# Loads behind a gate per tile, and another order in the second group, in a pooled-attention and expert-mixture kernel

## The chip, the core and the metric

The kernel runs on one core of a Trainium2 chip. The core has a matrix engine (TensorE, PE in the profile; its weight loads are shown as PEld), a vector engine (VectorE, DVE), a scalar engine (ScalarE, ACT), GpSimd (POOL) and SyncE (SP). Each works through its own list of instructions in order. Transfers between the chip's memory (DRAM) and the on-chip memory are made by 16 DMA engines, for which SP and POOL each issue work on a queue of their own. The metric is the device time of one execution in microseconds (us); lower is better.

## The reference

Eight batches of eight heads; 576 tokens of 64 numbers for each head. Keys and values are averaged over groups of 8 neighbouring tokens (72 pooled rows for a head), and every query attends to the 72 pooled rows of its head. The result, 4608 tokens of 512 numbers, goes through four small networks (512 to 1024 to 512), whose outputs are added with a token's own weights.

```python
k_p = k.reshape(B, H, Sp, pool, D).mean(axis=3)          # B 8, H 8, Sp 72, pool 8, D 64
v_p = v.reshape(B, H, Sp, pool, D).mean(axis=3)
scores = scale * np.matmul(q, k_p.transpose(0, 1, 3, 2))
scores = scores - np.max(scores, axis=-1, keepdims=True)
attn = np.exp(scores)
attn = attn / (np.sum(attn, axis=-1, keepdims=True) + 1e-09)
x = np.matmul(attn, v_p)                                 # then (4608, 512)
p = domain_probs / (domain_probs.sum(-1, keepdims=True) + 1e-09)
for e in range(4):
    h = np.maximum(x @ w1[e], 0.0)
    out += p[:, e:e + 1] * (h @ w2[e])
```

## The kernel before

**Tiles and steps.** The tokens are cut into 36 tiles of 128 (`t`), four tiles make a group (`g`, 512 tokens, nine groups). The networks run group by group and expert by expert: 36 steps `s = 4 g + e`. A step has 12 slots. In a slot TensorE does either two of the eight column blocks of the first matrix product of the *next* step (`up`, line 422; slots 0 and 1 of each three do one block each) or the second product of one tile of *this* step (`down`, line 454; the third slot), whose result VectorE weights and adds up (`collect`, line 466). After four experts the tile's sum is written out by SP (line 484).

**Attention beside it.** What a tile needs before its group's first step is hung into the slots by a hand-written plan: `at(slot, function, ...)` (line 490) puts a call behind the slot's products, and the final loop (line 588) calls what a slot has, in the order in which it was put there. There is no scheduler: each engine gets its instructions in exactly this order. `plan_tile` (line 501) hangs up the stages of one tile, and `plan_batch` (line 493) those of a batch's keys and values, with the batch's own loads `load_k` and `load_v` for the batch two later. From tile 8 on (group 2, called the body here) a tile's base slot is `(4 g - 5 + i) * 12`, so tiles follow each other 12 slots apart.

**Stages of a tile** in the body, with the slot counted from its base: `turn_q` (-6) turns the queries (`qT`) by a DMA transpose on SP; `scores` (0) is the product with the pooled keys on TensorE (line 306); `less_max` (0) on VectorE (lines 317 and 319); `expo` (+1) on ScalarE (line 329) writes `attn`; `attn_T` (+1) turns it (`attnT`) by a DMA transpose on SP (line 367); `sums` (+2) on VectorE (line 349 on); `context` (+6) is the product with the pooled values on TensorE (line 385), which VectorE scales into `x_sb` (line 391), and which SP turns into `xT` by a DMA transpose (line 405). `by_dma(t)` (line 284) tells body tiles, which turn by DMA, from tiles 0 to 7, which turn on TensorE with copies out of PSUM by ScalarE or VectorE (lines 296, 300, 371, 372).

**Stages of a batch**: `prep_k` folds the keys and pads them on VectorE (lines 225, 232, 240), `prep_kT` turns them four slots later, `prep_v` folds the values (lines 225, 232, 270) eight slots later. Two buffers each hold the raw keys and values.

**Loads.** All loads of queries, keys, values and weights are issued by POOL (lines 79, 83, 107, 115, 121), in the order of the calls. Loads convert from 32 to 16 bits on the way. A load waits only until its buffer is free: a key buffer until VectorE has folded the old keys, a query buffer (there are eight) until the old queries have been turned. POOL therefore runs ahead of the plan, and loads of the body start whenever the last one's buffer comes free. A load of keys or of values is two DMA issues, one of 512 rows and one of 64; a load of queries is one, or two where the tile lies over the border of two batches.

**Group 1** (tiles 4 to 7) is planned by itself, while the weights of the experts are still coming in: batch 1 from slot 10 on, tiles at slots 13, 17, 21 and 25.

Of the kernel before, what the change touches and what calls it, by code (L numbers as in the profile page):

```python
# [12 lines left out]
BF16 = mybir.dt.bfloat16  # L13
# [4 lines left out]
def kernel(  # L18
# [10 lines left out]
    nc = tc.nc  # L29

    B, H, S, D = q.shape
# [10 lines left out]
    TPG = G // P  # L42
    NT = NTOK // P
# [9 lines left out]
    const = ctx.enter_context(tc.tile_pool(name="const", bufs=1))  # L53
# [38 lines left out]
    def segments(t0, n):  # L92
        segs = []
        t = t0
        while t < t0 + n:
            b = t // S
            end = min(t0 + n, (b + 1) * S)
            segs.append((b, t - b * S, end - t, t - t0))
            t = end
        return segs  # L100
# [19 lines left out]
    def load_w2(e):  # L120
# [8 lines left out]
        out=dp0[:], in_=moe_domain_probs[0:G].rearrange("(p c) e -> p c e", c=TPG)  # L129
# [4 lines left out]
        out=dpr[:], in_=moe_domain_probs[G:NTOK].rearrange("(t p) e -> t p e", p=P)  # L134
# [7 lines left out]
        out=qg[:], in_=q[0][:, 0:G, :].rearrange("h (p c) d -> p h c d", c=TPG)  # L142
# [4 lines left out]
    for sign, base in ((1, 0), (-1, SP - 1)):  # L147
        nc.gpsimd.affine_select(
            out=own[:], in_=own[:], compare_op=ALU.is_ge, fill=0.0,
            base=base, channel_multiplier=sign,  # L150
# [8 lines left out]
    for c in range(TPG):  # L159
# [21 lines left out]
        out=p_sb[:, :, 0:TPG].rearrange("p e c -> p c e"), in0=dp0[:],  # L181
# [5 lines left out]
    for t in attn:  # L187
# [5 lines left out]
        out=mask_v[:].rearrange("p a z y d -> p (a z y) d"),  # L193
        in_=own[:].rearrange("p a z y -> p (a z y)").unsqueeze(2).to_broadcast(
            [P, NPAIR * 4, D]
        ),
# [3 lines left out]
        out=mask_k[:, 1:NPAIR], in0=mask_v[:, 1:NPAIR, 0], in1=mask_v[:, 0:NPAIR - 1, 1]  # L200
# [64 lines left out]
    def prep_v2(b):  # L265
        fold(vraw[b % 2], 0, NB, 2)
        s = last_fold(vraw[b % 2], "v")
        vbd[b] = prep.tile([P, NPAIR, 2, 2, D], BF16, name="vbd")
        for z in range(2):
            nc.vector.tensor_tensor(  # L270
                out=vbd[b][:, :, z],
                in0=s[:, z:z + NPAIR].unsqueeze(2).to_broadcast([P, NPAIR, 2, D]),
                in1=mask_v[:, :, z], op=ALU.mult,
            )
# [9 lines left out]
    def by_dma(t):  # L284
        return t >= 2 * TPG

    def turn_q(t):
        qT[t] = soft.tile([P, NPAIR, P], BF16, name="qT")
        if by_dma(t):
            nc.sync.dma_start_transpose(  # L290
                out=qT[t][:], in_=qrow[t][:].rearrange("p h d -> p (h d)")
            )
            return
        ps = ps_t.tile([P, NPAIR, P], BF16, tag="t", name="qT_ps")
        for pair in range(NPAIR):
            nc.tensor.transpose(
                ps[:, pair, :],
                qrow[t][:, 2 * pair:2 * pair + 2].rearrange("p h d -> p (h d)"), ident[:],
            )
        nc.scalar.copy(out=qT[t][:], in_=ps[:])  # L300
# [26 lines left out]
    def expo(t):  # L327
        if by_dma(t):
            nc.scalar.activation(  # L329
                out=attn[t % 2][:, 0:ROWS].rearrange("p (h j) -> p h j", j=SP),  # L330
                in_=st[t][:].rearrange("p g h j -> p (g h) j"),
                func=ACT.Exp, scale=EXP_SCALE,
            )
            return
        e_sb = soft.tile([P, H, SP], F32, name="e_sb")
        nc.scalar.activation(
            out=e_sb[:], in_=st[t][:].rearrange("p g h j -> p (g h) j"),
            func=ACT.Exp, scale=EXP_SCALE,
        )
        st[t] = e_sb  # L340

    rss = {}

    def sums(t):
        e = st[t][:]
# [15 lines left out]
            op0=ALU.mult, op1=ALU.mult,  # L361
        )

    def attn_T(t, copy=nc.vector.tensor_copy):
        attnT[t] = soft.tile([P, NB, P], BF16, name="attnT")
        if by_dma(t):
            nc.sync.dma_start_transpose(out=attnT[t][:], in_=attn[t % 2][:])
            return
        ps = ps_t.tile([P, NB, P], BF16, tag="t", name="at_ps")
        for i in range(NB):  # L370
            nc.tensor.transpose(ps[:, i, :], attn[t % 2][:, i * P:(i + 1) * P], ident[:])
        copy(out=attnT[t][:], in_=ps[:])
# [5 lines left out]
    def context_rows(t):  # L378
        ps = ps_t.tile([P, DM], F32, tag="t", name="x_ps")
        for b, _, n, at in segments(t * P, P):  # L380
            flat = vbd[b][:].rearrange("p a z y d -> p (a z y d)")
            for i in range(NB):
                c0, c1 = max(0, 4 * i - 1), min(4 * NPAIR, 4 * i + 2)
                h0 = max(0, 2 * i - 1)
                nc.tensor.matmul(  # L385
                    ps[at:at + n, h0 * D:(h0 + c1 - c0) * D],
                    lhsT=attnT[t][:, i, at:at + n], rhs=flat[:, c0 * D:c1 * D],
                    start=(i == 0), stop=(i == NB - 1), skip_group_check=True,
                )
        x_sb = soft.tile([P, DM], BF16, name="x_sb")  # L390
        nc.vector.scalar_tensor_tensor(  # L391
            out=x_sb[:].rearrange("p (h d) -> p h d", d=D),
            in0=ps[:].rearrange("p (h d) -> p h d", d=D), scalar=V_MEAN,
            in1=rss[t][:].unsqueeze(2).to_broadcast([P, H, D]),
            op0=ALU.mult, op1=ALU.mult,
        )
        return x_sb

    def context(t):
        g, col = t // TPG, (t % TPG) * P  # L400
        if t % TPG == 0:
            xT[g] = grp.tile([P, KC, G], BF16, name="xT")
        if by_dma(t):
            x_sb = context_rows(t)
            nc.sync.dma_start_transpose(out=xT[g][:, :, col:col + P], in_=x_sb[:])
            return
        ps = ps_t.tile([P, KC, P], F32, tag="t", name="x_ps")
        for pair in range(NPAIR):
            for b, _, n, at in segments(t * P, P):
                for z in range(2):  # L410
                    nc.tensor.matmul(  # L411
                        ps[:, pair, at:at + n],
                        lhsT=vbd[b][:, pair, z].rearrange("p y d -> p (y d)"),
                        rhs=attnT[t][:, pair + z, at:at + n],
                        start=(z == 0), stop=(z == 1),
                    )
        nc.scalar.copy(out=xT[g][:, :, col:col + P], in_=ps[:])
# [69 lines left out]
    SLOTS = 12  # L487
    plan = {}

    def at(slot, fn, *args):  # L490
        plan.setdefault(slot, []).append((fn, args))

    def plan_batch(b, slot):
        at(slot, prep_k, b)
        at(slot + 4, prep_kT, b)
        at(slot + 8, prep_v, b)
        if b + 2 < B:
            at(slot + 8, load_k, b + 2)
            at(slot + 8, load_v, b + 2)

    def plan_tile(t, slot, turn=0):
        exp, norm, move, sum_v = (3, 4, 3, 8) if by_dma(t) else (4, 5, 7, 9)
        if t + TPG < NT:
            at(slot, load_q, t + TPG)
        at(slot + turn, turn_q, t)
        at(slot + 2, scores, t)
        at(slot + 2, less_max, t)
        at(slot + exp, expo, t)
        at(slot + move, attn_T, t)
        at(slot + norm, sums if by_dma(t) else normalise, t)  # L510
        at(slot + sum_v, context, t)

    at(SLOTS - 4, domain_probs)
    plan_batch(1, SLOTS - 2)
    for i, slot in enumerate((1, 5, 9, 13)):
        plan_tile(TPG + i, SLOTS + slot)
    done_batches = 2
    for g in range(2, NG):
        for i in range(TPG):
            t = g * TPG + i  # L520
            base = (E * g - 5 + i) * SLOTS
            last_b = ((t + 1) * P - 1) // S
            if last_b >= done_batches:
                plan_batch(last_b, base - 13)
                done_batches += 1
            plan_tile(t, base - 2, -4)


    def split_q(c):
# [3 lines left out]
    def idle_products(n):  # L533
        ps = ps_o.tile([P, DM], F32, name="o_ps")
        for _ in range(n):
            nc.tensor.matmul(ps[:], lhsT=still[:, 0:P], rhs=still[:], start=True, stop=True)
# [17 lines left out]
    idle_products(5)  # L554
    normalise(0)
    prep_v2(0)
    attn_T(0, nc.scalar.copy)
    idle_products(2)
    context(0)
    less_max(1)  # L560
    expo(1)
# [5 lines left out]
    for t in range(1, TPG):  # L567
        if t == 1:
            turn_q(3)
        attn_T(t, nc.scalar.copy)  # L570
        if t + 1 < TPG:
            expo(t + 1)
        down(0, t - 1, 0, FB // 2)
        context(t)
        if t == 1:
            scores(3)
        down(0, t - 1, FB // 2, FB)
        up_tile(0, t)
        if t + 1 < TPG:
            normalise(t + 1)  # L580
        if t == 1:
            less_max(3)
        collect(0, t - 1)
# [4 lines left out]
    for s in range(NSTEP):  # L588
        for slot in range(SLOTS):
            part, i = slot % 3, slot // 3  # L590
# [39 lines left out]
```

## Time and profile before

| what | value |
|---|---|
| median of 3 runs | 569.9 us (569.69 to 571.6) |
| profiled execution | 573.24 us |
| its span, first to last instruction | 571.5 us |
| mean granted TensorE clock | 0.994 |
| busy share of PE, DVE, ACT, POOL | 95%, 47%, 36%, 11% |
| TensorE waits for attnT by DMA | 11.9 us, 6 times |
| TensorE waits for qT by DMA | 1.3 us, once |
| query loads in the span | 36 issues of 864 ns on POOL |
| DMA to landing, qT (min, median, max) | 2.4, 2.4, 7.7 us |
| DMA to landing, attnT (min, median, max) | 2.6, 2.6, 7.2 us |

A line of a timeline gives the start, the duration, the engine, the source line, the operation, what it writes and reads, and in brackets how long the engine had been idle and what it then waited for. SPq and POOLq are the queues on which DMA work is issued; the duration of a DMA issue is not that of the transfer, whose landing is given apart. A line of waits gives the total, the number and the longest. The granted clock is the share of TensorE's full clock that the chip let through.

### The profile page before, as it was taken

How to read it: one execution, taken by the hardware profiler on the slowest of the kernel's cores; microseconds unless marked ns; L12 is line 12 of the kernel's file. 1: busy time of each engine (PE TensorE's matmuls, PEld its weight loads, DVE VectorE, ACT ScalarE, POOL GpSimd, SP SyncE). 2: the span in 40 equal slices, each digit the busy share in tenths (PEclk: the TensorE clock that was granted, in tenths of full speed). 3: DMA queues.
4: the chain of work that ended last, by engine and by line, in shares of the span. 5: the costliest groups of instructions: out<-in, count | busy, mean ns of one | idle time of the engine just before them, and what ended most of it. 6: DMA issues, size and time to landing. Idle time of an engine off the chain costs nothing.

```text
span 571.5 us, 7185 instructions
## 1 busy us (share of the span) xinstructions
PE 540.4 (95%) x2888; PEld 259.2 (45%) x2888; DVE 269.2 (47%) x462; ACT 208.0 (36%) x347; POOL 64.2 (11%) x93
## 2 busy tenths in 40 slices
PE   3899898899898999899989999999999999999997
PEld 1564444344443444344444444444444444444443
DVE  4855865344552444544473444654465444422223
ACT  1564442233332333233333333333333333333330
POOL 7225303100040000300022000000000000000000
PEclk9999999899998999999999999999999999999999
DMA  9999998911592123781359243322221221111001
GB/s 140 207 203 200 197 110 135 121 22 30 98 160 37 30 31 104 106 86 31 86 102 108 36 75 74 50 38 68 68 42 31 59 76 30 31 34 50 1 0 73
DMA packets 111232, 45.43 MB, mean 79 GB/s; under 512 B 88128, under 2 KB 106560, under 8 KB 111200
## 3 DMA queue, kind: packets, MB, share of 16 engines
q0 software_dynamic: 52512, 22.55, 32.9%
q1 hardware_dynamic: 58688, 22.44, 17.2%
q8 instruction: 22, 0.36, 0.3%
q14 instruction: 10, 0.08, 0.0%
HBM read 45.16 MB, written 9.44 MB: 96 GB/s over the span
## 4 chain that ended last, share of the span: by engine, by line
PE 82%; DMA 8%; DVE 6%; issue 1%; ACT 1%; POOL 0%; POOLq 0%
PE o_ps L461 39%; PE h_ps L428 37%; DMA attnT<-attn 6%; PE x_ps L385 2%; PE sc L306 1%; DMA qg<-in_q_dram 1%; DMA qT<-qrow 1%; DVE mx L317 1%; DVE d_sb L319 1%; PE h_ps L444 1%; DVE kraw L225 1%; ACT attn L329 1%; PE x_ps L411 1%; DVE attn L357 1%; DVE es L349 0%
## 5 line engine op out<-in xcount | busy, mean ns | idle before, releaser
L432 ACT ACTIVATE h_sb<-h_ps 128x512 bf16<-128x512 f32 x280 | 166.4, 596 | 313.1 <-PE h_ps L428 313.1
L428 PE MATMUL h_ps<-xT,w 128*128 128x512 bf16 x1120 | 275.6, 380 | 0.0
L461 PE MATMUL o_ps<-w,h_sb 128*128 128x512 bf16 x1152 | 273.9, 381 | 0.0
L461 PEld LDWEIGHTS <-h_sb 128*128 128x128 bf16 x1152 | 112.8, 98 | 135.1 <-issue 3.6
L476 DVE SCALAR_TENSOR_TENSOR acc<-o_ps,p_sb,acc 128x512 f32<-128x512 f32 x108 | 81.0, 750 | 183.1 <-PE o_ps L461 183.1
L428 PEld LDWEIGHTS <-w 128*128 128x128 bf16 x1120 | 106.1, 98 | 116.9 <-issue 0.6
L472 DVE TENSOR_SCALAR acc<-o_ps,p_sb 128x512 f32<-128x512 f32 x36 | 27.0, 750 | 61.4 <-PE o_ps L461 61.4
L107 POOL DMA_DIRECT2D qrow<-in_q_dram x36 | 30.4, 864 | 83.2 <-DMA qT<-qrow 53.0
L317 DVE TENSOR_REDUCE mx<-sc 128x8 f32<-128x576 f32 x36 | 27.2, 755 | 12.1 <-PE sc L306 12.1
L391 DVE SCALAR_TENSOR_TENSOR x_sb<-x_ps,rs 128x512 bf16<-128x512 f32 x28 | 19.4, 691 | 26.2 <-PE x_ps L385 26.2
L319 DVE TENSOR_TENSOR d_sb<-sc,mx 128x576 f32<-128x576 f32 x36 | 27.3, 758 | 1.2
L79 POOL DMA_DIRECT2D kraw<-in_k_dram x9 | 6.8, 759 | 170.7 <-DVE k_sum L232 168.3
L385 PE MATMUL x_ps<-vbd,attnT 128*128 128x192 bf16 (+5 forms) x155 | 14.6, 234 | 11.9 <-DMA attnT<-attn 11.9
L329 ACT ACTIVATE attn<-d_sb 128x576 bf16<-128x576 f32 x28 | 19.1, 682 | 13.4 <-DVE d_sb L319 10.9
L349 DVE TENSOR_REDUCE es<-attn 128x8 f32<-128x576 bf16 x28 | 20.9, 746 | 0.5
L385 PEld LDWEIGHTS <-attnT 128*128 128x128 bf16 (+1 forms) x155 | 11.5, 101 | 20.5 <-DMA attnT<-attn 15.3
L306 PE MATMUL sc<-kT,qT 128*128 128x144 bf16 (+1 forms) x160 | 15.6, 232 | 1.6 <-DMA qT<-qrow 1.3
L306 PEld LDWEIGHTS <-qT 128*128 128x128 bf16 (+1 forms) x160 | 11.5, 102 | 11.4 <-DMA qT<-qrow 1.8
L225 DVE TENSOR_TENSOR kraw<-kraw 128x1280 bf16<-128x1280 bf16 (+5 forms) x18 | 10.8, 599 | 3.5 <-DMA kraw<-in_k_dram 3.2
L79 POOL DMA_DIRECT2D vraw<-in_v_dram x8 | 6.2, 773 | 39.0 <-DVE v_sum L232 35.5
L225 DVE TENSOR_TENSOR vraw<-vraw 128x1280 bf16<-128x1280 bf16 (+1 forms) x16 | 10.4, 653 | 0.2
L255 PE MATMUL kT_ps<-ident,kpad 128*128 128x128 bf16 x10 | 1.2, 264 | 9.2 <-DVE kpad L240 9.2
(61 smaller groups left out, 145.9 us busy)
## 6 DMA issues: line engine op xcount, KB each, us to landing
out_dram<-acc SPq DMA_DIRECT2D x36, 256.0 KB, 2.1
vraw<-in_v_dram POOLq DMA_DIRECT2D x8, 512.0 KB, 7.6
w<-in_moe_w_dram POOLq DMA_DIRECT2D x8, 512.0 KB, 16.0
w<-in_moe_w_dram POOLq DMA_DIRECT2D x4, 1024.0 KB, 16.8
kraw<-in_k_dram POOLq DMA_DIRECT2D x7, 512.0 KB, 6.0
qrow<-in_q_dram POOLq DMA_DIRECT2D x28, 128.0 KB, 8.0
kraw<-in_k_dram POOLq DMA_DIRECT2D x2, 256.0 KB, 4.4
kraw<-in_k_dram POOLq DMA_DIRECT2D x8, 64.0 KB, 5.6
```

The lines of the kernel that those rows point to most:

```text
L107: nc.gpsimd.dma_start(out=qrow[t][at:at + n], in_=q[b][:, tok:tok + n, :].rearrange("h p d -> p h d"),)
L225: nc.vector.tensor_add(out=rows[:, i0:i1, 0:w], in0=rows[:, i0:i1, 0:w], in1=rows[:, i0:i1, w:2 * w],)
L306: nc.tensor.matmul(sc[at:at + n, pair // 2, (pair % 2) * PW:(pair % 2 + 1) * PW], lhsT=qT[t][:, pair, at:at + n], rhs=kT[b][:].rearrange(" ...
L317: nc.vector.reduce_max(out=mx[:], in_=view, axis=AX.X)
L319: nc.vector.tensor_tensor(out=d_sb[:], in0=view, in1=mx[:].unsqueeze(3).to_broadcast([P, 2, 4, SP]), op=ALU.subtract,)
L329: nc.scalar.activation(out=attn[t % 2][:, 0:ROWS].rearrange("p (h j) -> p h j", j=SP), in_=st[t][:].rearrange("p g h j -> p (g h) j"), fun ...
L385: nc.tensor.matmul(ps[at:at + n, h0 * D:(h0 + c1 - c0) * D], lhsT=attnT[t][:, i, at:at + n], rhs=flat[:, c0 * D:c1 * D], start=(i == 0), s ...
L428: nc.tensor.matmul(ps[:], lhsT=w1_sb[e][:, kc, fb * P:(fb + 1) * P], rhs=xT[g][:, kc, :], start=(kc == 0), stop=(kc == KC - 1),)
L432: nc.scalar.activation(out=hs[s][:, fb, :], in_=ps[:], func=ACT.Relu)
L461: nc.tensor.matmul(ps[:], lhsT=hs[s][:, fb, i * P:(i + 1) * P], rhs=w2_sb[e][:, fb, :], start=(fb == 0), stop=(fb == FB - 1),)
L472: nc.vector.tensor_scalar_mul(out=accs[t][:], in0=ps[:], scalar1=p_sb[:, e, t:t + 1])
L476: nc.vector.scalar_tensor_tensor(out=accs[t][:], in0=ps[:], scalar=p_sb[:, e, t:t + 1], in1=accs[t][:], op0=ALU.mult, op1=ALU.add,)
```

## The change

- **A gate for each body tile.** After `context(t)`, POOL copies one element of that tile's `x_sb` into a scrap tile (`gate`). Since POOL works in order, loads called after it are issued only when `x_sb` is there.
- **Loads behind it.** In the body `load_q(t + 4)` is called behind the gate of tile `t` (slot +6) and not at the tile's slot -2. `load_k` and `load_v` of batches 4 to 7 are taken out of `plan_batch`; they go to a list, and each tile's gate lets one of them follow its query load.
- **Group 1.** Tiles are planned at slots 12, 16, 20 and 24 (one earlier) with `attn_T` and `context` one slot later within the tile, so that these two stay in the same slots; queries of tiles 5 to 7 are turned one slot ahead; batch 1's keys are turned at slot 12 and its values folded at slot 12 (14 and 18 before). The loads of batch 3's keys and values are called at slot 12, ahead of the queries of tiles 8 and 9. `attnT` of these tiles is copied by ScalarE and not by VectorE.
- **Tile 8** has its queries turned on TensorE instead of by DMA, two slots before its scores.

```diff
     def turn_q(t):
-        if by_dma(t):
+        if by_dma(t - 1):
...
+    gated = const.tile([1, 1], BF16, name="gated")
...
-    def attn_T(t, copy=nc.vector.tensor_copy):
+    def attn_T(t, copy=nc.scalar.copy):
...
-            x_sb = context_rows(t)
+            x_sb = x_sbs[t] = context_rows(t)
...
         at(slot + 8, prep_v, b)
-        if b + 2 < B:
-            at(slot + 8, load_k, b + 2)
-            at(slot + 8, load_v, b + 2)
+
+    def gate(t):
+        nc.gpsimd.tensor_copy(out=gated[:], in_=x_sbs.pop(t)[0:1, 0:1])
 
     def plan_tile(t, slot, turn=0):
-        exp, norm, move, sum_v = (3, 4, 3, 8) if by_dma(t) else (4, 5, 7, 9)
-        if t + TPG < NT:
+        exp, norm, move, sum_v = (3, 4, 3, 8) if by_dma(t) else (4, 5, 8, 10)
+        if t + TPG < NT and not by_dma(t):
             at(slot, load_q, t + TPG)
...
         at(slot + sum_v, context, t)
+        if by_dma(t):
+            at(slot + sum_v, gate, t)
+            if t + TPG < NT:
+                at(slot + sum_v, load_q, t + TPG)
 
-    plan_batch(1, SLOTS - 2)
-    for i, slot in enumerate((1, 5, 9, 13)):
-        plan_tile(TPG + i, SLOTS + slot)
-    done_batches = 2
+    at(SLOTS - 2, prep_k, 1)
+    at(SLOTS, prep_kT, 1)
+    at(SLOTS, prep_v, 1)
+    at(SLOTS, load_k, 3)
+    at(SLOTS, load_v, 3)
+    for i, slot in enumerate((0, 4, 8, 12)):
+        plan_tile(TPG + i, SLOTS + slot, -1 if i else 0)
+    done_batches, waiting = 2, []
...
                 plan_batch(last_b, base - 13)
                 done_batches += 1
-            plan_tile(t, base - 2, -4)
+                if last_b + 2 < B:
+                    waiting += [(load_k, last_b + 2), (load_v, last_b + 2)]
+            plan_tile(t, base - 2, -4 if t > 2 * TPG else 0)
+            if waiting:
+                load, b = waiting.pop(0)
+                at(base + 6, load, b)
```

More of the change, by code (lines that the diff above doesn't have):

```diff
@@ L340, in expo @@
         st[t] = e_sb
-    rss = {}
+    rss, x_sbs = {}, {}
+    gated = const.tile([1, 1], BF16, name="gated")
     def sums(t):
@@ L556 @@
     prep_v2(0)
-    attn_T(0, nc.scalar.copy)
+    attn_T(0)
     idle_products(2)
@@ L569 @@
             turn_q(3)
-        attn_T(t, nc.scalar.copy)
+        attn_T(t)
         if t + 1 < TPG:
```

## The prediction

> **What bounds the kernel now.** I read the page's shares first, then the chain that ended last, then TensorE's waits, then the stretches in which they lie. From the page:
>
> ```profile
> PE 540.4 (95%) x2888; PEld 259.2 (45%) x2888; DVE 269.2 (47%) x462; ACT 208.0 (36%) x347; POOL 64.2 (11%) x93
> PE 82%; DMA 8%; DVE 6%; issue 1%; ACT 1%; POOL 0%; POOLq 0%
> ```
>
> The chain is TensorE work, broken by pieces of DMA. A step of TensorE is at its floor (8 matmuls in 1.73 us on the chain), so only what it waits for can be won. Its waits, from 27 to 96 us (group 1 and the first body tile), then from 96 to 320 us:
>
> ```profile
> PE at_ps L371 <- DVE attn L357: 2.4, 2, 1.6
> PE x_ps L385 <- DMA attnT<-attn: 1.7, 1, 1.7
> ...
> PE x_ps L385 <- DMA attnT<-attn: 10.2, 5, 2.7
> PE sc L306 <- DMA qT<-qrow: 1.3, 1, 1.3
> ```
>
> After 305 us none is left, to the end. The transfers waited for are transposes on SP's queue that met loads on POOL's. One such meeting in the timeline, then in the DMA issues of the same stretch (count, KB, us to landing):
>
> ```profile
> 288.10 0.76 POOL L79 DMA_DIRECT2D kraw<-in_k_dram  x1 [43.95 <-DVE k_sum L232]
> 290.53 1.20 SPq L367 DMA_TRANSPOSE attnT<-attn  x1
> 295.08 0.51 PE L385 MATMUL x_ps<-vbd,attnT 128*128 128x128 bf16 x5 [1.66 <-DMA attnT<-attn]
> ...
> kraw<-in_k_dram POOLq DMA_DIRECT2D x1, 512.0 KB, 5.9
> kraw<-in_k_dram POOLq DMA_DIRECT2D x1, 64.0 KB, 5.5
> attnT<-attn SPq DMA_TRANSPOSE x1, 4.5
> ```
>
> The keys are issued when their buffer is free, the transpose 2.4 us later, and it lands after 4.5 us; the median of the 28 is 2.6. Two waits cost twice. Windows around the waits at 107.6 us (2.66 us) and 171.7 us (2.45 us); to be seen are PE busy and, after POOL, the granted clock:
>
> ```profile
> 106.90:110.31 3.41, 0.75 (x5) 0.16 (x3) 0.62 (x1) 0.60 (x1) 0.00 (x0) 1.00 0.88 68
> 110.31:113.72 3.41, 3.41 (x12) 1.54 (x13) 0.69 (x1) 0.60 (x1) 0.00 (x0) 0.50 0.20 39
> 171.75:175.16 3.41, 1.02 (x13) 0.70 (x14) 0.38 (x1) 0.58 (x1) 0.00 (x0) 1.00 0.47 58
> 175.16:178.58 3.42, 3.42 (x10) 1.19 (x9) 0.31 (x1) 0.60 (x1) 0.00 (x0) 0.50 0.36 73
> ```
>
> Each was followed by 3.41 us at clock 0.50, which loses 1.7 us of work; the wait of 1.88 us at 233.8 was not.
>
> **The change, part by part.** The sum is made against the profiled execution, 573.24 us (span 571.5, 1.7 around it). The median of the three runs, 569.9, is 3.3 less; I carry that difference over.
>
> *Loads taken away from attnT.* The eight loads of keys and values of batches 4 to 7, and the query bursts beside them, now start after a tile's x_sb. The body's waits are 1.7 + 10.2 + 1.3 = 13.2 us and the two slow windows 3.4: 16.6 us go. attnT is not late next: it is issued 8.8 us after x_sb ends, and the loads are down after 7.6 (both below).
>
> *The gate itself.* 28 one-element copies on POOL: the nearest rows are its memsets (0.10 us) and its selects (0.43), so 3 to 12 us in all, on an engine busy for 11%. Queued behind each gate are only loads. A query load is for a tile four ahead, over 40 us later at 14.4 us a tile; the first gated keys come after tile 9 and are folded for tile 18. So the delay is hidden; without that cover it would show as waits of DVE on kraw or of SP on qrow. x_sb's buffer is rewritten two tiles after its gate, so DVE does not wait. I take nothing.
>
> *What the loads meet now.* In that slot SP issues xT(t) and then qT(t+1). A clean tile:
>
> ```profile
> 326.35 0.69 DVE L391 SCALAR_TENSOR_TENSOR x_sb<-x_ps,rs 128x512 bf16<-128x512 f32 x1 [0.44 <-PE x_ps L385]
> 327.06 1.19 SPq L405 DMA_TRANSPOSE xT<-x_sb  x1
> 328.42 1.19 SPq L290 DMA_TRANSPOSE qT<-qrow  x1
> ...
> 333.05 0.41 PE L306 MATMUL sc<-kT,qT 128*128 128x144 bf16 x4
> ...
> 335.80 2.13 SPq L367 DMA_TRANSPOSE attnT<-attn  x1
> ```
>
> Call the end of x_sb (327.04) zero. qT is issued at 1.4, scores want it at 6.0: it may take 4.6 us, and takes 2.4 clean. POOL starts 0.3 after a DVE result (kraw follows k_sum so), plus 0.1 for the gate: queries issue at 0.45 and, with 0.88 an issue, keys or values at 1.35, just before qT. A query load alone lands 3.5 after its issue (row of 331.37), at 4.0. Transposes caught by a load landed 0.7 after the load's tail (above: 290.53 + 4.5 = 295.0, against 294.3 for the tail, issued at 288.84). That gives qT 4.7, in time: the 16 tiles with a query load only cost nothing. Their cover is 1.3 us; gone, they would cost as rival C.
>
> For the 8 tiles with keys or values, no row shows this order, so bounds. Low: qT's data slips through ahead of the load, as where values came 0.6 us after qT: it landed after 4.0 to 4.1 us three times (6.1 the fourth time, waiting 1.3). Below 4.6 there is no wait, and below nothing is impossible, since an early qT starts no score earlier. High: qT lands 0.7 after the load's tail, which comes 6.2 after the load's issue: 6.9 after its own issue, a wait of 2.3. I take the middle, 5.5, a wait of 0.85: it lies between the 4.0 and 6.1 of the nearest rows plus the query load ahead, which those lacked. 8 x 0.85 = 6.8 us.
>
> Two rows show why I don't take an end. From 231 to 233 us, with a transpose issued at 230.90, SP's queue moved nothing beside a load of keys; from 75 to 77 us the two queues shared:
>
> ```profile
> q0 software_dynamic: 371, 0.38, 121.8%
> ...
> q0 software_dynamic: 398, 0.28, 89.5%
> q1 hardware_dynamic: 388, 0.10, 36.7%
> ```
>
> The Trainium skill, "DMA: Bandwidth & Descriptors", section "Queues, rings and completion order", says that each DMA engine goes round the queues packet by packet. By that alone qT would get half the engines, land an estimated 1 us late, at 3.4, and the sum would lose its 6.8 us of new waits. The row of 231 to 233 speaks against it for the first microseconds.
>
> *Group 1.* Batch 1's values are folded six slots earlier, tiles' scores one slot earlier, attnT's transposes in the same slots (20, 24, 28, 32). The two waits for attn, 1.62 and 0.77 us, came while DVE was busy with those folds and with the next tile's softmax. Bounds: 2.4 us won if both go; 1.2 lost if the copy of attnT, now on ACT (690 ns for 481, four times, plus a relu of 0.6 ahead of one), is late. I take 2.0 won, since a slot of matmuls stands between copy and use either way.
>
> *qT(8) on TensorE.* Four transposes more (0.39 us, row of 48.78), one copy on ACT (0.58) beside matmuls, one DMA transpose less on SP, which had landed 7.7 us after its issue and was not waited for. 0.4 us lost. Keys and values of batch 3 now precede queries 8 and 9 on POOL; those land near 77 to 78 us instead of 71 and 72, tile 8 is turned near 81. Nothing.
>
> Sum: 573.2 - 16.6 - 2.0 + 0.4 + 6.8 = 561.8; less 3.3, **558.5 us**.
>
> **The rivals.** 0.3% is about what a measurement of this kernel can tell from no change.
> - *A, the forecast*: waits of 0.2 to 1.5 us in eight places: 1.6 to 12 us instead of 6.8, so 553 to 564. Chance 0.47.
> - *B, hidden*: qT always gets through: 569.9 - 18.2 = 551.7. For it the three rows of 4.0 to 4.1; against it that they had no query load ahead. 0.22.
> - *C, slower*: the wait for qT replaces that for attnT. In eight places qT waits for the load's end, 2.3 us each: 18.4, with no clock lost 570.1; but 2.45 us idle in one window was enough to halve the clock, so half of them may cost 1.7 more: 577. It decides from 18.2 / 8 = 2.3 us a tile, a qT landing 6.9 us after its issue. For it the row of 231 to 233 us, against it that of 75 to 77 us. 0.25.
> - *D, no difference*: waits merely move, one for one: 569.9. 0.06.
>
> "TensorE: Matmul & The Clock Gate", section "Why this matters for your kernels", allows idle gaps up to about 3 us. By it C would lose no clock and end at 570; the rows above show 2.45 us to be too long.
>
> **How the numbers follow.** Faster: A, B and a part of C: 0.71; same: D and a part of C: 0.06; slower: 0.23. The range from 551 to 576 leaves out B's lower edge and C with most clocks lost. A's own range is 553 to 564.
>
> **What would show it.** Right: no x_ps wait on attnT in the body, attnT landing in 2.6 us throughout; sc waits on qT at tiles 10, 11, 14, 15, 19, 20, 23 and 24 and nowhere else, 0.2 to 1.5 us each; clock 0.50 after none; at_ps waits under 0.5 us. Wrong: qT above 6.5 us in most of those tiles with slow windows behind them; waits in tiles with a query load only; waits of DVE on kraw, which would mean that gates delay loads too far.

## The result and the profile after

The changed kernel takes 563.8 us (median of 6 runs, 561.25 to 564.33) against 569.65 of the kernel before beside it: a ratio of 0.9885, 95% interval 0.9861 to 0.9909. A second measurement on another chip gave 0.9857 (0.9826 to 0.9888). The forecast was 558.5 us, with a range from 551 to 576: the gain is 5.9 us (8.1 on the second chip) where 11.4 were forecast. The profiled execution is 563.63 us with a span of 561.7, 9.8 less than the 571.5 before.

The chain that ended last, from the page of the changed kernel:

```profile
PE 88%; DMA 7%; DVE 2%; issue 1%; ACT 1%; POOL 0%; DVEq 0%; POOLq 0%
PE o_ps L462 41%; PE h_ps L429 40%; DMA qT<-qrow 5%; PE sc L306 2%; PE x_ps L386 2%; PE h_ps L445 2%; DMA kraw<-in_k_dram 1%; DMA attnT<-attn 1%; PE x_ps L412 1%; DVE kraw L225 0%; ACT attnT L373 0%; PE qT_ps L296 0%; PE o_ps L551 0%; POOL kraw L79 0%; DVE mx L317 0%
```

The transfer in the chain is now `qT` (5%), where before it was `attnT` (6%, with `qT` at 1%). TensorE's waits in the changed kernel from 27 to 325 us (after that there is none), as total, number and longest:

```profile
PE sc L306 <- DMA qT<-qrow: 6.8, 5, 2.2
PE x_ps L386 <- DMA attnT<-attn: 1.5, 1, 1.5
```

Before, the same two were 1.3 and 11.9, with 2.4 for `attn` in group 1. One of the five new waits in the timeline of the changed kernel (the values of batch 5, behind tile 14's gate):

```profile
177.80 1.19 SPq L406 DMA_TRANSPOSE xT<-x_sb  x1
...
177.91 0.18 POOL L501 COPY gated<-x_sb 1x1 bf16<-1x1 bf16 x1 [12.27 <-DVE x_sb L392]
...
178.42 0.92 POOL L107 DMA_DIRECT2D qrow<-in_q_dram  x1 [0.33 <-issue]
...
179.09 1.21 SPq L290 DMA_TRANSPOSE qT<-qrow  x1
...
179.32 0.76 POOL L79 DMA_DIRECT2D vraw<-in_v_dram  x1
...
186.10 0.42 PE L306 MATMUL sc<-kT,qT 128*128 128x144 bf16 x4 [2.22 <-DMA qT<-qrow]
```

and the DMA issues of 177 to 181 us, the last number being the time to landing:

```profile
vraw<-in_v_dram POOLq DMA_DIRECT2D x1, 512.0 KB, 8.2
...
qT<-qrow SPq DMA_TRANSPOSE x1, 7.0
```

The values, 512 KB and a rest of 64 KB, are issued 0.23 us after `qT`, and `qT` takes 7.0 us instead of a clean 2.4. Five of the eight tiles with such a load wait (14, 15, 20, 23 and 24: 0.3, 2.2, 1.6, 0.6 and 2.1 us); the other three don't.

**Where the 9.8 us of span went.** Gone: 13.2 us of body waits, two half-clock windows (3.4 us of work) and 2.4 us in group 1, together 19.0. Back: 6.8 + 1.5 us of waits, 0.8 us before the first step of group 0 is collected (48.1 us instead of 47.3; a half-clock window at 20.9 us lies there in this execution), some 0.2 for tile 8's turn (0.22 us on the chain). 19.0 - 9.3 = 9.7.

### The profile page after: what moved, and what is told of

Same layout as the page of the kernel before. It is cut to its first block, busy times and chain, and to the rows that moved or that the text cites. A ratio compares the mean times of both kernels' runs of the same rounds, so it can differ in the third digit from the quotient of the medians.

```text
span 561.7 us, 7210 instructions
## 1 busy us (share of the span) xinstructions
PE 533.6 (95%) x2837; PEld 259.4 (46%) x2892; DVE 267.7 (48%) x458; ACT 210.8 (38%) x352; POOL 71.8 (13%) x121
## 4 chain that ended last, share of the span: by engine, by line
PE 88%; DMA 7%; DVE 2%; issue 1%; ACT 1%; POOL 0%; DVEq 0%; POOLq 0%
PE o_ps L462 41%; PE h_ps L429 40%; DMA qT<-qrow 5%; PE sc L306 2%; PE x_ps L386 2%; PE h_ps L445 2%; DMA kraw<-in_k_dram 1%; DMA attnT<-attn 1%; PE x_ps L412 1%; DVE kraw L225 0%; ACT attnT L373 0%; PE qT_ps L296 0%; PE o_ps L551 0%; POOL kraw L79 0%; DVE mx L317 0%
## 5 line engine op out<-in xcount | busy, mean ns | idle before, releaser
L429 PE MATMUL h_ps<-xT,w 128*128 128x512 bf16 x1088 | 271.8, 379 | 1.5
L462 PE MATMUL o_ps<-w,h_sb 128*128 128x512 bf16 x1129 | 269.9, 379 | 1.4
L501 POOL COPY gated<-x_sb 1x1 bf16<-1x1 bf16 x28 | 7.8, 278 | 370.6 <-DVE x_sb L392 370.6
L329 ACT ACTIVATE attn<-d_sb 128x576 bf16<-128x576 f32 x28 | 19.1, 682 | 13.2 <-DVE d_sb L319 10.8
L350 DVE TENSOR_REDUCE es<-attn 128x8 f32<-128x576 bf16 x28 | 20.9, 745 | 0.5
L225 DVE TENSOR_TENSOR kraw<-kraw 128x1280 bf16<-128x1280 bf16 (+5 forms) x18 | 10.8, 599 | 3.0 <-DMA kraw<-in_k_dram 2.7
L445 PE MATMUL h_ps<-xT,w 128*128 128x128 bf16 x128 | 9.3, 240 | 0.7 <-ACT xT L418 0.7
```

The costliest lines, as they stand in the source:

```text
L225: nc.vector.tensor_add(out=rows[:, i0:i1, 0:w], in0=rows[:, i0:i1, 0:w], in1=rows[:, i0:i1, w:2 * w],)
L350: nc.vector.reduce_sum(out=es[:], in_=e, axis=AX.X)
L429: nc.tensor.matmul(ps[:], lhsT=w1_sb[e][:, kc, fb * P:(fb + 1) * P], rhs=xT[g][:, kc, :], start=(kc == 0), stop=(kc == KC - 1),)
L462: nc.tensor.matmul(ps[:], lhsT=hs[s][:, fb, i * P:(i + 1) * P], rhs=w2_sb[e][:, fb, :], start=(fb == 0), stop=(fb == FB - 1),)
```

## The experiments

Theory W ("window"): scores wait where the packets of a keys or values load begin while `qT`'s are still to come; a little later, and `qT` slips through. Rival T ("tail"): a `qT` that meets a load waits for that load's end, whenever it was issued. A second question came up with the result: what the wait of 1.5 us for `attnT` in tile 17 is, where no load is under way. (The expectations below call this tile 18: it is the tenth body tile, and the body begins with tile 8.)

All runs; the waits are TensorE's from 27 us on, in the profiled execution, in us. Ratios are to the kernel before on the same chip.

| run | median us | ratio (95%) | sc on qT | x_ps on attnT | at_ps on attn |
|---|---|---|---|---|---|
| before (first profile) | 569.65 | 1 | 1.3 | 11.9 | 2.4 |
| changed | 563.8 | 0.9885 (0.9861 to 0.9909) | 6.8 | 1.5 | 0 |
| changed, second chip | 561.52 | 0.9857 (0.9826 to 0.9888) | 3.8 | 1.6 | 0 |
| pause of three copies | 554.98 | 0.9746 (0.9721 to 0.9772) | 0 | 1.3 | 0 |
| pause of six copies | 554.61 | 0.9717 (0.9692 to 0.9741) | 0 | 1.2 | 0 |
| keys and values behind attnT | 555.61 | 0.9760 (0.9735 to 0.9785) | 2.3 | 1.1 | 0 |
| without the eight loads | 555.0 | 0.9751 (0.9726 to 0.9776) | 0 | 1.5 | 0 |
| keys and values first | 582.74 | 1.0204 (1.0157 to 1.0252) | 20.6 | 1.6 | 0 |
| gates alone | 560.67 | 0.9832 (0.9799 to 0.9866) | 6.6 | 0 | 1.5 |
| group 1 alone | 570.7 | 0.9997 (0.9972 to 1.0022) | 0 | 13.7 | 0 |
| pause of three, 15 idle products | 555.18 | 0.9726 (0.9695 to 0.9757) | 1.9 | 0 | 0 |
| changed, tile 8 by DMA | 560.3 | 0.9841 (0.9799 to 0.9882) | 5.0 | 0 | 0 |
| gates alone, pause of six | 554.78 | 0.9738 (0.9710 to 0.9766) | 0 | 0 | 1.8 |
| tile 8 by DMA, pause of six | 553.01 | 0.9689 (0.9657 to 0.9722) | 0 | 0 | 0 |

### A pause between query load and keys or values

```diff
+    pause_t = const.tile([1, 2], BF16, name="pause_t")
+    nc.vector.memset(pause_t[:], 0.0)
...
+    def pause(n):
+        for _ in range(n):
+            nc.gpsimd.tensor_copy(out=pause_t[:, 1:2], in_=pause_t[:, 0:1])
...
                 load, b = waiting.pop(0)
+                at(base + 6, pause, 3)
                 at(base + 6, load, b)
```

> The changed kernel, with three one-element copies on POOL (0.28 us each in the group of the gates, so 0.5 to 0.8 us) between a gate's query load and its load of keys or values. Theory W (window): the scores wait because the load's packets begin while qT's packets are still to come; where the load was issued 0.67 us or more after qT, qT landed in 4.1 to 4.5 us and nothing waited, where it was issued 0.2 us after, qT took 5.1 to 7.0. So qT lands in under 4.6 us in all eight tiles, the waits of scores fall from 6.8 us to under 1, and the time is about 6 us below the changed kernel's 563.8: 557 to 558.5. Rival T (tail): a qT that meets a load waits for the load's end; the end comes 0.5 to 0.8 us later, so the waits grow by 2 to 6 us: 566 to 570.

Measured 554.98 us, 2 us below the range that W gave. The same place as above, in the timeline with three copies:

```profile
178.22 1.21 SPq L290 DMA_TRANSPOSE qT<-qrow  x1
...
178.35 0.65 POOL L507 COPY pause_t<-pause_t 1x1 bf16<-1x1 bf16 x3
...
179.06 0.75 POOL L79 DMA_DIRECT2D vraw<-in_v_dram  x1
...
182.84 0.41 PE L306 MATMUL sc<-kT,qT 128*128 128x144 bf16 x4
```

and its DMA issues there:

```profile
vraw<-in_v_dram POOLq DMA_DIRECT2D x1, 512.0 KB, 6.6
...
qT<-qrow SPq DMA_TRANSPOSE x1, 3.5
```

The load comes 0.84 us after `qT` instead of 0.23, and `qT` lands in 3.5 us instead of 7.0. Over the eight tiles it lands in 3.4 to 4.2. T, which wanted it later, falls. The pause itself costs POOL 0.65 us here, and no new wait of TensorE comes with it.

The packets on SP's queue show what happens between. A `qT` is 544 packets; alone (the clean tile of the kernel before, issued at 328.42 us) all of them move between 1.0 and 2.5 us after its issue. In tile 15 of the changed kernel, from 1 to 3 us after the issue and in the 4 us after that:

```profile
q1 hardware_dynamic: 457, 0.12, 30.6%
...
q1 hardware_dynamic: 87, 0.01, 2.6%
```

and with three copies, from 1 to 3 us after the issue:

```profile
q1 hardware_dynamic: 544, 0.13, 32.3%
```

Most of `qT` gets through in time either way. Without the pause its last 87 packets are drawn out beside the load's, and with it none is left for the load to delay.

### A pause twice as long

The same with six copies.

> As the run with three copies between query load and keys or values, with six copies, so the load comes some 1.4 us or more after qT instead of 0.8. Theory W: qT lands in 3.4 to 4.2 us in the eight tiles, scores wait for nothing; the load's tail now ends near 10 us after x_sb, the next attnT is issued 8.8 us after it and would land at 11.4 anyhow, so nothing waits there either: within 1 us of the 555.0 with three copies. Rival: the load now reaches into attnT, which lands 1 to 2 us late with waits of x_ps as in the kernel before: 559 to 565.

Measured 554.61 us: the loads come 1.5 to 2.6 us after `qT`, which lands in 3.5 to 4.2 us, and no `attnT` outside tile 17 is waited for (two land in 3.0 us). Between 0.8 and 2.6 us the delay makes no difference: there is a window, not an optimum.

### Keys and values ahead of the query load

```diff
-    def plan_tile(t, slot, turn=0):
+    def plan_tile(t, slot, turn=0, first=None):
...
         if by_dma(t):
             at(slot + sum_v, gate, t)
+            if first:
+                at(slot + sum_v, *first)
             if t + TPG < NT:
                 at(slot + sum_v, load_q, t + TPG)
...
-            plan_tile(t, base - 2, -4 if t > 2 * TPG else 0)
-            if waiting:
-                load, b = waiting.pop(0)
-                at(base + 6, load, b)
+            first = waiting.pop(0) if waiting else None
+            plan_tile(t, base - 2, -4 if t > 2 * TPG else 0, first)
```

> The changed kernel, with the load of keys or values ahead of the query load behind the same gate, so issued 0.9 us earlier, some 0.7 us before qT. Theory W: its packets now begin before qT's in all eight tiles and qT waits for most of the load, 7 us or more after its issue, waits of 2 to 3 us in eight places: 16 to 24 us instead of 6.8, 573 to 582 us with what the clock loses. Theory T: the load's end comes 0.9 us earlier, the query load's end 0.9 us later; qT's wait is set by whichever is last, much the same as now: 562 to 566 us.

Measured 582.74 us: slower than the kernel before. One of its waits in the timeline:

```profile
184.87 0.76 POOL L79 DMA_DIRECT2D vraw<-in_v_dram  x1 [0.27 <-issue]
...
185.61 1.21 SPq L290 DMA_TRANSPOSE qT<-qrow  x1
...
193.15 0.56 PE L306 MATMUL sc<-kT,qT 128*128 128x144 bf16 x4 [2.75 <-DMA qT<-qrow]
```

With the load 0.7 to 0.8 us ahead of `qT`, `qT` lands 6.7 to 7.7 us after its issue, 0.8 to 1.4 us after the load's tail, in all eight tiles. The waits are 20.6 us (0.3 of them in a ninth tile), and three of them cost a half-clock window besides. The windows around the wait above, with the granted clock 1.00 and then 0.50:

```profile
189.88:193.30 3.42, 0.67 (x6) 0.18 (x5) 0.45 (x1) 0.60 (x1) 0.00 (x0) 1.00 1.96 128
193.30:196.71 3.41, 3.41 (x12) 1.42 (x11) 1.52 (x2) 1.17 (x2) 0.00 (x0) 0.50 0.00 0
```

None of the 544 packets of this `qT` moves in the first 4.5 us after its issue. W holds, and the time lies just above its range. T's rule does describe this order, but not the one of the change: 0.9 us of the load's issue decide between the two. (The query load moves in this run too, from some 0.7 us ahead of `qT` to some 0.5 us behind it.)

Put together, by the issue of keys or values against that of `qT` (negative: ahead), over the eight tiles of each run:

| load's issue after qT's | runs | qT's landing after its issue |
|---|---|---|
| -0.8 to -0.7 us | keys and values first | 6.7 to 7.7 us |
| -0.02 and 0.07 us | gates alone; pause of three, 15 idle products (one tile each) | 7.3 and 6.0 us |
| 0.16 to 0.23 us | changed, both chips (five tiles of eight) | 5.0 to 7.0 us |
| 0.53 to 0.65 us | before and group 1 alone, no query load ahead (four tiles each) | 3.9 to 4.2 us, once 6.1 |
| 0.67 to 0.73 us | changed, both chips (three tiles of eight) | 3.9 to 4.5 us |
| 0.8 to 1.9 us | pause of three | 3.4 to 4.2 us |
| 1.5 to 2.6 us | pause of six | 3.5 to 4.2 us |

The three tiles of the changed kernel that wait for nothing are those where keys and values happened to come half a microsecond later: two whose query load lies over a border of batches and takes two issues, and one whose query load is issued 1.15 us after `x_sb` and not 0.65. The delay of the load is not all: with 0.16 to 0.23 us the landing still lies anywhere from 5.0 to 7.0 us, and what makes this difference stays open.

### Keys and values behind attnT

```diff
+    gated2 = const.tile([1, 1], BF16, name="gated2")
...
+    def gate_attn(t):
+        nc.gpsimd.tensor_copy(out=gated2[:], in_=attnT[t][0:1, 0, 0:1])
...
+            if waiting:
+                load, b = waiting.pop(0)
+                at(base + 5, gate_attn, t)
+                at(base + 5, load, b)
             plan_tile(t, base - 2, -4 if t > 2 * TPG else 0)
-            if waiting:
-                load, b = waiting.pop(0)
-                at(base + 6, load, b)
```

> The changed kernel, with the loads of keys and values behind a gate of their own that reads one element of the tile's attnT, which lands 3.1 us before x_sb is done; the query load stays behind the gate on x_sb. The load of keys or values is then issued some 2.5 us before x_sb and its tail lands 6.2 us later, near 3.7 us after x_sb, the query load near 4.5. Theory T: qT lands 0.7 us after the last load, near 5.2, and scores want it at 6.0: no wait, 557 to 558.5, and xT lands late (4 to 5 us instead of 2.4) without anybody waiting. Theory W: the same time if qT finds the queue empty after 4.5 us; if the packets of both loads keep qT behind them, waits of 0.5 to 1 us stay in the eight tiles: 561 to 565.

Measured 555.61 us. The loads come 4.1 to 4.6 us ahead of `qT`. In seven tiles they end 1.3 to 2.6 us after its issue, and it lands in 4.0 to 4.9 us. In one it took 6.7 us (a load that itself took 8.3), a wait of 1.9. The load can lie on either side of `qT`, but not across it.

### Without the eight loads

```diff
                 load, b = waiting.pop(0)
-                at(base + 6, load, b)
+                pass
```

Batches 4 to 7 then fold what is left in the buffers.

> The changed kernel without the eight loads of keys and values of batches 4 to 7: these batches then fold what is left in the buffers, so their output is not the reference's; all other work is the same. It measures what the eight loads cost in their place. Theory (both W and T): no wait of scores on qT is left, qT lands in 3.5 to 4.7 us in every tile, and the time is 6.8 us less: 557 us. Rival: the waits do not come from these loads but from query loads or instruction fetches; then qT still lands late in some tiles and the time stays within 2 us of 563.8.

Measured 555.0 us, no wait of scores on `qT`. With the pause the loads are there and the time is the same, 554.98: in the window they cost nothing that can be measured.

### The two parts of the change

The gates alone (the turn of tile 8, group 1 and its copies as before):

> The kernel before with the gates and the loads behind them alone; group 1, the turn of tile 8's queries and the copies of attnT stay as before. Theory: the gates are the larger part; the body keeps the changed kernel's waits (scores 6 to 8 us in all, none for keys at attnT), group 1 keeps its two waits for attn of 2.4 us, and the time lies some 2 us above the changed kernel, 0.992 of the kernel before (0.989 to 0.996). Rival: group 1's order was worth nothing, 0.9885 as the changed kernel.

Measured 560.67 us, 0.9832, below what both the theory and its rival gave: not slower than the whole change, although group 1 waits 1.5 us for `attn`. It has no wait in tile 17. Group 1 alone:

> The kernel before with group 1 in the new order alone (with the loads of batch 3 ahead of queries 8 and 9, attnT copied by ScalarE and tile 8's queries turned on TensorE); the loads of the body are not gated. Theory: the two waits for attn in group 1 go, the waits of the body for attnT and qT stay at 11 to 15 us: 2 us less, 0.9965 of the kernel before (0.994 to 0.999). Rival: nothing is won (1.000), or the body's meetings of loads and transposes change with it and the time moves by more than 4 us either way.

Measured 0.9997. The waits for `attn` are gone, as expected, and yet nothing is won. Its waits from 27 us on:

```profile
PE x_ps L385 <- DMA attnT<-attn: 13.7, 6, 3.7
```

The longest is tile 17's, 3.68 us, where the kernel before waits 1.88 at the same tile; it is followed by a third half-clock window. So group 1's 2.4 us are there up to 230 us (that `x_ps` is due at 230.63 us instead of 233.79) and given back in one place. This is the tile of the unexplained wait. In both kernels its `attnT` meets a load of keys, whose tail comes 4.0 us after the issue of `attnT` before and 4.2 us here; `attnT` lands after 4.7 us before and after 6.5 us here.

### The wait of tile 17

In the timeline of the changed kernel:

```profile
219.34 1.21 SPq L368 DMA_TRANSPOSE attnT<-attn  x1
...
220.65 2.21 SPq L249 DMA_TRANSPOSE kT<-kpad  x1
```

The issue of the keys' transpose takes 2.21 us instead of some 1.23. The DMA queues of 219 to 222 us in the changed kernel, and the landing:

```profile
q8 instruction: 1, 0.02, 2.3%
...
attnT<-attn SPq DMA_TRANSPOSE x1, 4.3
```

A packet of 16 KB of instructions falls into the transfer. Such packets come every 250 or so instructions of TensorE (at 193.8, 221.3 and 249.6 us here); in both runs of the changed kernel one comes 2.0 us after the issue of this `attnT`. So, if they belong to fixed places of TensorE's program, a few instructions more or fewer of TensorE move them against the tiles. Fifteen idle products at the start, where TensorE waits 9.3 us for the first keys, put ahead of `prep_k(0)` in the run with three copies:

> As the run with three copies, with 15 idle products more (30 instructions of TensorE) at its start, where it waits 9.3 us for the first keys anyhow. Theory F: the wait of 1.1 to 1.6 us for attnT in tile 18, which stays in every run near 220 us, comes from a 16 KB instruction fetch, which returns every 256 or so instructions of TensorE and there falls into attnT's transfer; 30 instructions more move it some 3 us ahead of the transfer, attnT of tile 18 lands in 2.6 us or less instead of 4.1, its wait is gone, and the time is 1 to 1.5 us less than with three copies (553.5 to 554), unless the fetch meets another transfer that is waited for. Rival: the wait belongs to tile 18 itself (its keys' fold, its two batches), and stays at 1.3 us.

Measured 555.18 us, 0.9726 against 0.9746. Tile 17's wait is gone, but the profiled execution has another one:

```profile
PE sc L306 <- DMA qT<-qrow: 1.9, 1, 1.9
```

The packet now falls at 162.7 us into tile 13's `xT`, whose issue takes 2.02 us; `qT` is issued 0.8 us late, the keys 0.07 us after it, outside the window. The wait costs a half-clock window besides (at 171.3 us). The total hardly moves, since the fetch met another transfer. Turning tile 8 by DMA as before takes eight instructions of TensorE away:

```diff
-        if by_dma(t - 1):
+        if by_dma(t):
...
-            plan_tile(t, base - 2, -4 if t > 2 * TPG else 0)
+            plan_tile(t, base - 2, -4)
```

> The changed kernel with tile 8's queries turned by DMA as before, all else as changed. TensorE then has 8 instructions fewer (four transposes, four weight loads), so that its instruction fetches come 0.8 us later against the tiles. Theory F (the fetch that falls into tile 18's attnT makes its wait, and it fell there because the change added instructions): the wait of tile 18 shrinks below 0.7 us or goes, and the time is 0.4 (the turn) to 2 us less than that of the changed kernel. Rival: the turn of tile 8 is free either way and tile 18's wait stays, same time within 0.5 us.

Measured 560.3 us beside 561.52 for the changed kernel on the same chip, whose own expectation was:

> The changed kernel itself, beside variants of it on one chip. Expected: 0.986 to 0.991 of the kernel before; scores wait 4 to 8 us on qT in the tiles of keys and values; the wait of 1.1 to 1.6 us for attnT in tile 18 again.

Without tile 8's turn on TensorE, tile 17's wait is gone, and `attnT` there lands in 2.6 us:

```profile
attnT<-attn SPq DMA_TRANSPOSE x1, 2.6
```

The packet comes 3.7 us after the issue of `attnT` instead of 2.0. All profiles go the same way. In the seven in which the packet comes 1.8 to 2.1 us after the issue of this `attnT`, it lands in 3.9 to 4.5 us and is waited for; in the five in which it comes 2.3 us before or 3.6 to 3.9 us after, `attnT` lands in 2.4 to 2.6 us and is not. In the other two, the kernel before and group 1 alone, a load of keys is in the way as well. The packet comes 5.8 us after the issue before, when `attnT` has landed, and 4.3 us after it in group 1 alone, before it has. So the cause of the wait is shown where no load is under way. That the fetch also makes the longer wait of group 1 alone fits, but was not tested by itself. The medians' difference of 1.2 us is within their intervals (0.9799 to 0.9882 and 0.9826 to 0.9888); the wait's end is in the trace.

### Both fixed

Gates alone with six copies:

> The gates alone, with group 1 as before, and six copies on POOL between query load and keys or values. Theory: the scores' waits of 6.6 us go as they did with the whole change, no wait of tile 18 comes, and what stays is group 1's wait for attn, 1.5 to 2.4 us: 553.5 to 555, as good as the whole change with six copies (554.6), whose group 1 is 2 us faster and whose tile 18 waits 1.2 us. Rival: group 1's new order is worth its 2 us here: 556 to 557.

Measured 554.78 us, as the theory gave, with group 1's 1.8 us of waits left. The changed kernel with six copies and tile 8 by DMA:

> The changed kernel with tile 8's queries turned by DMA as before and six copies on POOL between query load and keys or values: group 1's new order with neither the scores' waits nor the fetch in tile 18. Theory: none of the waits is left from 27 us on but, at most, one of a fetch elsewhere, and group 1's order shows its 2 us: 552.5 to 553.5 us, 0.970 to 0.973 of the kernel before. Rival: group 1's order is worth nothing by itself, 554.5 to 555 as with the gates alone and six copies (554.8).

Measured 553.01 us, 0.9689 (0.9657 to 0.9722): no wait of TensorE at all from 27 us to the end of the profiled execution. This is the fastest version, 10.8 us below the changed kernel's 563.8. Group 1's order shows its worth in the trace, where the 1.8 us of waits of the gates alone are gone; the medians differ by 1.8 us too, but they are from two chips, and the intervals (0.9657 to 0.9722 and 0.9710 to 0.9766) just overlap.

## Why the prediction was right or wrong

- **Loads taken away from attnT**: right that no `attnT` was waited for because of a load, and that neither half-clock window behind such a wait came back. The size of the step was off: the tail of keys or values came 7.1 to 9.1 us after the load's issue, not 6.2, so in four tiles (10, 11, 14 and 19) it reached into the next `attnT`. Tile 19's landed in 4.0 us and was used 0.4 us later; a little more would have been a wait. The sign "attnT landing in 2.6 us throughout" was not met there, nor in tile 17.
- **The gate**: right that it costs nothing (7.8 us of POOL in 28 copies, no wait of DVE on keys, none of SP on queries). Its delay was taken a little short: the query load is issued 0.65 us after `x_sb` ends (177.77 to 178.42), not 0.45.
- **What the loads meet now**: right that the waits lie only in tiles with keys or values. That the sum agrees, 6.8 us forecast and 6.8 measured, is in part luck: the same kernel gave 3.8 on the second chip, and the single tiles are not as forecast. Eight were to wait 0.2 to 1.5 us; three waited for nothing, three 1.6 to 2.2 us. The mean landing of 5.4 us against 5.5 taken is made up of 4.1 to 4.5 us in three tiles and 5.1 to 7.0 in five. Between the two bounds the issue of the load decides, within some 0.5 us, and the gate was mis-timed by 0.2 us. With keys and values 0.05 us ahead of `qT`, as the sum had them, more would have been lost: 0.02 us ahead, in one tile of the gates alone, `qT` took 7.3 us. With keys and values 0.9 us earlier, rival C was the result: that run gave 20.6 us of waits and 582.7 us, where C said 577. Its point of decision, a `qT` of 6.9 us, was the right one.
- **Query loads only**: right, no wait in those 16 tiles. `qT` took 3.4 to 4.7 us there, so in the worst of them nothing of the cover was left.
- **Group 1**: 2.0 us taken, 2.4 us there in the waits. What the step missed is that the same edits move TensorE's instruction fetches against the tiles: 1.5 us were lost again at tile 17. In the run of group 1 alone all of the gain was lost at that tile. Of the turn of tile 8 only its own 0.4 us had been counted.
- **The carried-over difference**: the step that failed. The sum against the profiled execution, 561.8 us, is 1.8 below the 563.63 measured, of which the fetch is 1.5. The rest of the miss in the median, 558.5 against 563.8, is the 3.3 us taken off because the profile before stood that much above its median. The changed kernel's profile stands at its median (563.63 and 563.8). The profiled execution before had lost two half-clock windows at a mean granted clock of 0.994 (half of 3.41 us, of 571.5, is 0.003 for each). Of the 11 runs of it beside the first experiments, the five at 0.999 took 567.5 to 568.8 us, the six at 0.994 to 0.997 568.9 to 572.0. By their clock most runs had lost one such window or none, so a part of the 3.4 us that the sum took out was not in the median to begin with, and taking off 3.3 us more counted it twice in part.
- **The rule on queues**: the Trainium skill, "DMA: Bandwidth & Descriptors", section "Queues, rings and completion order", has the engines go round the queues packet by packet. By the estimate that the prediction made from it, no wait was to be expected. The runs agree where `qT` is issued 0.67 us or more ahead of the load, and in seven tiles of eight where it is issued 4 us behind it. A `qT` issued 0.7 us after a load of 576 KB waited for its end.

## What to carry to other kernels

A load that may be early is best put where no short transfer on the way to the bound engine is under way, and the place is a matter of half a microsecond: list, for each wait, what was issued within a microsecond of the late transfer on any queue. When both ends of a bound are far apart, look for what switches between them and time that, rather than take the middle. And carry a profile's sum over to a median only after the terms that differ from run to run, such as clock windows, are taken out of both.

## What the runs showed of the hardware that was not expected

- **Half-clock windows follow a grid.** In the record of the granted clock, windows of 3.41 us lie end to end, and one at 0.50 follows a window in which TensorE stood still long enough. Laid over that grid, 2.13 us of standing still inside one window cost the next (group 1 alone, wait at 168.6 us), also 2.23 and 2.62 (keys and values first, at 254.4 and 320.4), while 2.79 us in all did not where the grid cut it into 1.99 and 0.80 (keys and values first, at 273.2), nor 2.66 cut into two parts of some 1.3 (gates alone, at 303.8). The limit is not a sharp one: 1.95 us inside one window did cost the next in another run (15 idle products, at 168.5). The Trainium skill, "TensorE: Matmul & The Clock Gate", section "Why this matters for your kernels", has gaps of about 3 us as the limit. The runs differ: some 2 us in one window were enough.
- **Instruction fetches are transfers too.** A 16 KB packet of instructions, about every 250 instructions of TensorE, took 0.9 to 1.8 us of a DMA engine. Where it came some 2 us after the issue of tile 17's `attnT`, this landed after 3.9 to 4.5 us instead of 2.4 to 2.6. Where it comes counts: `attnT` of tile 24 in the changed kernel, with the packet 0.4 us after its issue, landed after 2.9 us.
